# One wo stripe loaded as 96 partitions over all DMA engines and four times 8 partitions over eight engines

## The chip, the cores and the metric

The kernel runs on one core of one Trainium2 chip. The metric is the device time of one execution in microseconds (us). Here "engine" means one of the core's 16 DMA engines, the units that move data between HBM and SBUF (the core's on-chip memory, addressed as 128 partitions); compute engines are called by name. A "row" is one contiguous packet that a DMA engine moves into one partition (in the trace a stripe is 128 packets of 9216 bytes).

## The reference

Two independent attention problems, A and B, of the same shape; the outputs are concatenated. Only the window of the last 4096 positions is read, so about 150 MB must come from HBM while the arithmetic is that of one token.

```python
B, Sq, D = 2, 1, 576
Hq, Hkv, Sk, Dh = 32, 16, 16384, 128          # W = 4096
q = (x @ wq).reshape(B, Sq, Hq, Dh).transpose(0, 2, 1, 3)
k = repeat(k_cache[:, :, Sk - W:, :], 2, axis=1)
v = repeat(v_cache[:, :, Sk - W:, :], 2, axis=1)
p = softmax(einsum("bhqd,bhkd->bhqk", q, k) * Dh ** -0.5)
o = einsum("bhqk,bhkd->bhqd", p, v)
out = o.transpose(0, 2, 1, 3).reshape(B, Sq, Hq * Dh) @ wo
```

## The kernel before

SyncE issues a fixed sequence of loads: both wq, then slabs of K and V of 4 MB each (128 partitions, 32 KB per partition) into four ring slots, and between them eight "stripes" of wo (1024 rows of the matrix, 128 partitions, 9216 bytes per partition) into two buffers. A load waits only for the last reader of its slot. The loads land in the order of issue (the first landings of four slabs queued one behind the other come at 34.42, 44.15, 53.87 and 63.57 us). The part that issues a stripe:

```python
ring = sb("ring", [128, NSLOT, SW], BF16)           # 4 x 32 KB per partition
wob  = sb("wob", [128, 2, 8, NOUT], BF16)           # 2 x 9216 bytes per partition
# ... cut ...
def issue(key):
    kind, i = key
    if kind == "W":
        P, gl = i // GP, i % GP
        sl = i % 2
        rows = probs[P][4][gl * 1024:(gl + 1) * 1024, :].rearrange("(p j) n -> p j n", j=8)
        deps = [proj_op[i - 2]] if i >= 2 else []
        cuts = [(0, 8, wo_sem[sl])]
        # ... cut: the last two stripes go in two and three column pieces ...
        stream_dma[key] = []
        for j0, j1, sm in cuts:
            def f(e, j0=j0, j1=j1, sm=sm):
                return e.dma_start(wob[:, sl, j0:j1, :].rearrange("p j n -> p (j n)"),
                                   rows[:, j0:j1, :].rearrange("p j n -> p (j n)")).then_inc(sm, 16)
            stream_dma[key].append((j0, j1, dma_op("sp", sm, 1, f, deps, "wo%d_%d" % (i, j0))))
        return
    # ... cut: the same for a slab of K or V into ring[:, r] ...
```

## Time and profile before

| | before |
|---|---|
| median, 6 runs beside the change | 363.61 us (363.37 to 366.12) |
| bytes read from HBM | 153.1 MB, 422 GB/s over the span |
| share of 16 DMA engines' time, SyncE's ring | 98.7% |
| TensorE / VectorE busy | 65% / 58% |
| 16 landings of the 432 KB piece of the last stripe | 357.76 to 359.92 us |

From the page of the kernel before: the span, compute busy times, the DMA share and rate in 40 slices (a 9 is 90% or more), the queue that SyncE feeds and one of the two that fetch instructions (packets, MB, share of 16 engines), the chain of waits by engine, and the full wo loads of problem A (KB each, median us from issue to landing).

```profile
span 362.4 us, 2626 instructions
...
PE 235.4 (65%) x1296; PEld 57.1 (16%) x928; DVE 211.9 (58%) x141; ACT 46.3 (13%) x80; POOL 21.9 (6%) x82
...
DMA  8999999999999999999999999999999999999996
GB/s 326 448 428 420 445 421 438 430 423 445 412 443 430 427 441 406 443 434 430 435 421 438 430 427 436 423 434 434 427 427 433 430 438 423 436 427 434 416 412 245
...
q1 hardware_dynamic: 6772, 153.10, 98.7%
q8 instruction: 8, 0.13, 0.1%
...
DMA 60%; DVE 24%; PE 8%; issue 6%; ACT 1%; SPq 0%; POOL 0%
...
wob<-in_A_wo_dram SPq DMA_DIRECT2D x4, 1152.0 KB, 30.8
```

The DMA engines are busy all the time and everything else has slack. So the time is bytes over rate, or, more exactly, what the slowest of the 16 engines needs, plus about 2.5 us of tail.

The stretches around stripe 1, which runs through the engines at 144 to 147 us. The columns are named in the first line: busy us (and instructions) of each compute engine, granted TensorE clock, DMA share and GB/s. Single lines of this view further down have the same columns.

```profile
core 0: us, PE busy (x) PEld busy (x) DVE busy (x) ACT busy (x) POOL busy (x), PEclk, DMA share, GB/s
130.00:141.00 11.00, 7.14 (x25) 1.51 (x14) 9.26 (x8) 0.00 (x0) 0.39 (x2) 0.84 1.00 430
141.00:152.00 11.00, 7.72 (x64) 2.22 (x48) 6.17 (x4) 5.01 (x8) 1.27 (x4) 0.96 1.03 436
152.00:163.00 11.00, 8.21 (x22) 1.46 (x11) 6.72 (x3) 0.00 (x0) 0.00 (x0) 0.66 1.00 429
163.00:350.00 187.00, 123.76 (x737) 32.48 (x568) 115.73 (x83) 25.47 (x41) 9.36 (x34) 0.85 1.00 429
```

Three steps of the chain of waits, in order of time (start, us, what): the same kind of slab takes 27 to 29 us from issue to landing every time, because two or three slabs are always queued ahead of it.

```profile
99.17 27.28 DMA ring<-in_A_k_cache_dram
...
139.24 28.85 DMA ring<-in_B_k_cache_dram
...
180.88 28.86 DMA ring<-in_B_k_cache_dram
```

The trace also has each DMA packet (start, duration, bytes; not the engine) and each landing on a semaphore, 16 for a load of 128 rows; each is read as one engine's share. From these records of the kernel before:

```
row of 32768 bytes   1.213 to 1.225 us (5th to 99th percentile)   26.9 GB/s
row of  9216 bytes   0.347 to 0.360 us (5th to 99th percentile)   26.4 GB/s
instruction fetch, 16384 bytes   8 packets of 1.02 to 1.10 us, at 47, 103, 144, 185, 226, 268, 310, 339 us
instruction fetch,  8192 bytes   3 packets of 0.31 to 0.33 us
landings of one slab on its 16 engines: spread 0.65 us (44.15 to 44.79) early, 2.20 us (347.43 to 349.63) late
```

The instruction fetches go through the same 16 engines as the data and put an engine about 1.05 us behind for the rest of the run: after the first one, at 47 us, the spread of a slab's landings goes from 0.64 to 1.67 us and stays there (1.69 us at 104 us) until the next fetch, at 103 us, has run. That is the imbalance that the change seems meant for.

### The profile page before, as it was taken

Reading aid. Unit: us, or ns where it says so; the run is one execution under the profiler, and the core shown is the slowest. Engines: PE = TensorE matmul, PEld = TensorE weight load, DVE = VectorE, ACT = ScalarE, POOL = GpSimd, SP = SyncE. Lnnn points to the kernel's source line nnn. Section 1 sums busy time; section 2 is a strip of 40 time slices with the busy share of each in tenths; the row PEclk is TensorE's granted clock in tenths of the full one; section 3 lists DMA queues with packets and bytes.
Section 4 is the critical chain, followed back from the end, with each engine's and each line's share of the span. In section 5 each row is a group of like instructions: output and inputs, shape, how many; then the busy total and the mean of one; then the engine's idle time right before and its main releaser. Section 6 shows DMA issues by size and latency. Waiting matters only on the chain.

```text
span 362.4 us, 2626 instructions
## 1 busy us (share of the span) xinstructions
PE 235.4 (65%) x1296; PEld 57.1 (16%) x928; DVE 211.9 (58%) x141; ACT 46.3 (13%) x80; POOL 21.9 (6%) x82
## 2 busy tenths in 40 slices
PE   0397698566666856665786737657686646668566
PEld 0010111112111211111121201212121111212212
DVE  0201899495949093954939185582929467493622
ACT  1002100140041000500032000500005000400500
POOL 3100101100010001000010000100010001000000
PEclk9999699969897889868698977998888898978879
DMA  8999999999999999999999999999999999999996
GB/s 326 448 428 420 445 421 438 430 423 445 412 443 430 427 441 406 443 434 430 435 421 438 430 427 436 423 434 434 427 427 433 430 438 423 436 427 434 416 412 245
DMA packets 6803, 153.26 MB, mean 423 GB/s; under 512 B 764, under 2 KB 904, under 8 KB 1544
## 3 DMA queue, kind: packets, MB, share of 16 engines
q1 hardware_dynamic: 6772, 153.10, 98.7%
q8 instruction: 8, 0.13, 0.1%
q14 instruction: 3, 0.02, 0.0%
q10 hardware_dynamic: 20, 0.01, 0.0%
HBM read 153.10 MB, written 0.00 MB: 422 GB/s over the span
## 4 chain that ended last, share of the span: by engine, by line
DMA 60%; DVE 24%; PE 8%; issue 6%; ACT 1%; SPq 0%; POOL 0%
DMA ring<-in_B_k_cache_dram 32%; DVE xt L427 15%; DMA ring<-in_A_k_cache_dram 14%; DMA ring<-in_B_v_cache_dram 8%; DMA ring<-in_B_wq_dram 7%; PE st L244 2%; DVE oR L559 2%; DVE mx L461 2%; PE st L453 2%; DVE pT L500 2%; PE pj L244 2%; DVE tmp L552 2%; ACT pR L491 1%; PE pj L608 1%; DVE oP L583 1%
## 5 line engine op out<-in xcount | busy, mean ns | idle before, releaser
L453 PE MATMUL st<-xt,zq 128*128 128x512 bf16 x256 | 122.5, 478 | 92.2 <-DVE xt L427 92.2
L427 DVE STREAM_TRANSPOSE xt<-ring 128x4096 f32<-128x4096 f32 x32 | 141.6, 4430 | 39.1 <-DMA ring<-in_A_k_cache_dram 23.8
L244 PE MATMUL st<-xt,zq 128*128 128x512 bf16 x256 | 121.2, 474 | 0.0
L491 ACT ACTIVATE pR<-st,bias 128x512 bf16<-128x512 f32 x32 | 40.1, 1422 | 226.7 <-DVE bias L484 226.7
L453 PEld LDWEIGHTS st<-xt,zq 128*128 128x128 bf16 x256 | 29.0, 113 | 215.1 <-DVE xt L427 109.0
L530 PE MATMUL ot<-ring,pT 128*32 128x512 bf16 x512 | 32.6, 396 | 6.4 <-DMA ring<-in_B_v_cache_dram 6.4
L484 DVE SCALAR_TENSOR_TENSOR bias<-vmask,tb,offm 128x4 f32<-128x4 f32 x8 | 1.8, 223 | 36.6 <-PE tb L481 36.6
L514 DVE TENSOR_REDUCE ssum<-tb 128x2 f32<-128x8 f32 x8 | 1.3, 161 | 37.1 <-PE tb L511 37.1
L500 DVE STREAM_TRANSPOSE pT<-pR 128x2048 bf16<-128x2048 bf16 x8 | 18.4, 2304 | 1.2 <-ACT pR L491 1.2
L419 POOL TENSOR_TENSOR zq<-qs,bmask 128x64 bf16<-128x64 bf16 x32 | 8.7, 294 | 165.8 <-PE st L244 143.6
L552 DVE SCALAR_TENSOR_TENSOR tmp<-ot,rsb,dmask 128x512 f32<-128x512 f32 x16 | 11.5, 717 | 8.7 <-PE ot L530 8.7
L559 DVE TENSOR_REDUCE oR<-tmp 128x128 f32<-128x512 f32 x15 | 15.7, 1044 | 0.5
L530 PEld LDWEIGHTS ot<-ring,pT 128*32 128x32 bf16 x512 | 12.4, 99 | 21.7 <-DMA ring<-in_B_v_cache_dram 8.5
L608 PE MATMUL pj<-wob,oP 128*2 128x288 bf16 x64 | 15.1, 286 | 0.0
L244 PE MATMUL pj<-wob,oP 128*2 128x288 bf16 x56 | 14.0, 286 | 0.0
L244 PE MATMUL pj<-ring,pT 128*32 128x512 bf16 x36 | 11.5, 402 | 0.0
L254 PE MATMUL tb<-ident_b,pR 8*128 8x8 bf16 x9 | 0.7, 198 | 14.2 <-DVE pR L215 14.2
L461 DVE TENSOR_REDUCE mx<-st 128x2 f32<-128x1024 f32 x8 | 9.7, 1214 | 0.0
L491 ACT ACTIVATION_READ_ACCUMULATOR pR<-st,bias 128x1 f32 x32 | 9.1, 285 | 0.0
L275 PE MATMUL ot<-ring,pT 128*32 128x512 bf16 x18 | 7.3, 405 | 1.3 <-DMA ring<-in_B_wq_dram 0.9
L215 DVE TENSOR_TENSOR pR<-tmp,hmask 8x1152 bf16<-8x1152 bf16 x1 | 1.3, 1347 | 11.2 <-DMA tmp<-in_B_x_dram 11.2
L565 PE MATMUL tb<-oR,selx 128*128 128x256 f32 (+1 forms) x18 | 5.9, 408 | 2.7 <-DVE ssum L514 1.5
(64 smaller groups left out, 68.8 us busy)
## 6 DMA issues: line engine op xcount, KB each, us to landing
ring<-in_A_k_cache_dram SPq DMA_DIRECT2D x8, 4096.0 KB, 27.9
ring<-in_A_v_cache_dram SPq DMA_DIRECT2D x8, 4096.0 KB, 30.5
ring<-in_B_k_cache_dram SPq DMA_DIRECT2D x8, 4096.0 KB, 28.9
ring<-in_B_v_cache_dram SPq DMA_DIRECT2D x7, 4096.0 KB, 30.5
ring<-in_A_wq_dram SPq DMA_DIRECT2D x1, 4608.0 KB, 13.6
ring<-in_B_wq_dram SPq DMA_DIRECT2D x1, 4608.0 KB, 24.1
wob<-in_A_wo_dram SPq DMA_DIRECT2D x4, 1152.0 KB, 30.8
wob<-in_B_wo_dram SPq DMA_DIRECT2D x2, 1152.0 KB, 30.2
```

Source lines behind the costliest of these rows:

```text
L244: return e.add_instruction(mybir.InstMatmult(name=nc.get_next_instruction_name(), engine=mybir.EngineType.PE, ins=[e.lower_ap(mv_), e.lowe ...
L275: last = e.matmul(QB[c], wt, mv_, start=first, stop=True, skip_group_check=True)
L419: last = e.tensor_tensor(dst, src, msk, ALU.mult)
L427: Xop[(t, jh)] = dve(lambda e: e.transpose(xt[:, jh, :].bitcast(FP32).rearrange("p (kp x kt) -> p x kp kt", kp=2, kt=2), ring[:, r, jh * H ...
L453: last = e.matmul(ob, wt, mv_, start=first, stop=True, skip_group_check=True)
L461: ch[(G, "max")] = dve(lambda e: e.tensor_reduce(mx[:], st[:, :].rearrange("p (x t) -> p t x", t=2), AX.X, ALU.max), [Sop[(2 * G + 1, 1)]] ...
L491: last = e.activation(pR[:].rearrange("p (x k) -> p k x", k=4)[:, kv, :], st[:, :].rearrange("p (x t) -> p t x", t=2)[:, kv % 2, :], ACTF.Exp,
L500: pT_op[G] = dve(lambda e: e.transpose(pT[:, v, :].rearrange("p (w j q) -> p j w q", w=4, q=8), pR[:].rearrange("p (j w q) -> p j w q", w= ...
L530: last = e.matmul(OTB[32 * c:32 * c + 32, :], pT[:, v, base + 32 * c:base + 32 * c + 32], ring[:, r, jj * 128:(jj + 4) * 128], start=rd == ...
L552: evac_op[i] = dve(lambda e: e.scalar_tensor_tensor(tv, o, rsb[:, v, b:b + 1], dm, ALU.mult, ALU.mult), deps, "ev%d" % i)
L559: ch[(G, "red%d" % b)] = dve(lambda e: e.tensor_reduce(oR[:, b, :], tmp[:].rearrange("p (j d) -> p d j", j=4), AX.X, ALU.add), [evac_op[i] ...
L608: last = e.matmul(PJ[h], wt, mv_, start=start and j == 0, stop=True, skip_group_check=True)
```

## The change

Stripe 1 is dealt unevenly: 6 rows to each of 16 engines and 4 more to each of eight, instead of 8 to each. That is an estimate from the landings, 16 for a load of 128 rows and eight for one of 8 rows (t1_tags), with each load taken as dealt evenly; no trace names the engine of a row. One half of the engines is relieved of two rows (0.69 us), the other half gets two more.

```diff
                 stream_dma[key] = []
+                if i == 1:
+                    halves = [(0, 96)] + [(96 + 8 * k, 104 + 8 * k) for k in range(4)]
+                    def f(e, sm=wo_sem[sl]):
+                        for p0, p1 in halves:
+                            last = e.dma_start(wob[p0:p1, sl, :, :].rearrange("p j n -> p (j n)"),
+                                               rows[p0:p1, :, :].rearrange("p j n -> p (j n)")).then_inc(sm, 16)
+                        return last
+                    stream_dma[key].append((0, 8, dma_op("sp", wo_sem[sl], len(halves), f, deps, "wo%d" % i)))
+                    return
                 for j0, j1, sm in cuts:
```

## The prediction

> **What bounds the kernel.** The DMA engines. The slice view shows DMA at 9 tenths nearly throughout; in the queue view SyncE's ring takes 98.7% of 16 engines' time. 153.1 MB in 362.4 us is 422 GB/s. Single packets agree: a 32 KB row takes 1.213 to 1.225 us (26.9 GB/s), a 9216-byte row of wo 0.347 to 0.36 us, each beginning as the last ends. The chain of waits is DMA for 60%; two or three 4 MB transfers are always outstanding (28 to 30 us to landing, 9.7 us of engine time each). So the time is that of the slowest of 16 engines, plus about 2.5 us of tail.
>
> **Imbalance.** Landings of a transfer on its 16 engines spread over 0.65 us at the start and over 2.15 us for the last wo piece (357.76 to 359.92 us). The growth comes from instruction fetches: eight packets of 16 KB, 1.02 to 1.10 us each, put one engine after another about 1.05 us behind for good; three of 8 KB cost 0.31 us each. From the phase of A's output transfer I infer that neither of the two engines it uses is among the eight.
>
> **What the change does.** Before: 8 rows per engine. After: 6 rows on each of 16 engines, then four more on eight of them. [...] plus and minus 2 x 0.347 = 0.69 us. [...] Four more issues (0.59 us each) hide in SyncE's 7 us wait for a slot.
>
> **The other side.** [...] Every engine is busy to the end, so lost time is not regained.
>
> **Prediction.** 366.6 us; range 363.4 to 371. [...] Faster by over 2%: 0.01; within 2%: 0.91; slower by over 2%: 0.08.
>
> **Right if:** rows of the four small transfers take well over 0.36 us (0.7 to 2), eight engines leave the stripe 3 to 6 us late, landings of later transfers spread over 4 to 6 us instead of 2 and the last landing is 2 to 5 us later with compute unchanged.
> **Wrong if:** those rows still take 0.35 us (then the final spread shrinks to about 1.5 us, the time by about 0.5); [...] or run-to-run variation (363.5 to 366.1) hides it all.

Where the text above is marked as cut, it rested on statements about the hardware that no trace or run here shows: which eight engines an 8-row load uses, and why its rows should take longer. The sum came to 366.6 us. It weighed two cases, both estimates: about 363.8 us (30%) if the rows of the small transfers keep their time, and 366 to 369 us (70%) if they slow each other. For the second, the author had the eight engines of the small transfers lose 3 to 5 us, less about 1 us that they were thought to have in hand. The guess (65%): the engines put behind by fetches are those which the small transfers leave alone; then the last landing was to fall by about 0.5 us, otherwise to come 0.7 us later.

(What the prediction calls "the last wo piece" is the 432 KB piece of the last stripe; a piece of 144 KB lands 0.36 us after it.)

## The result and the profile after

The changed kernel takes 368.76 us in the median of 6 runs (368.32 to 370.87), the kernel before 363.61 us. The ratio is 1.0136, 95% interval 1.0100 to 1.0171: slower, but within 2%. A ratio here is the mean time of one kernel's fast runs over that of the other's of the same rounds, so it is not quite the ratio of the medians quoted.

The same lines of the page after:

```profile
span 367.2 us, 2629 instructions
...
PE 233.9 (64%) x1295; PEld 57.0 (16%) x928; DVE 211.9 (58%) x141; ACT 46.3 (13%) x80; POOL 22.0 (6%) x82
...
DMA  8999999999999999999999999999999999999995
GB/s 322 450 428 421 436 452 403 453 421 439 421 444 414 443 421 355 301 446 414 444 408 454 414 450 421 441 414 446 418 415 449 436 421 446 412 446 421 418 413 224
...
q1 hardware_dynamic: 6804, 153.10, 98.6%
...
DMA 60%; DVE 23%; PE 8%; issue 6%; ACT 1%; SPq 0%; POOL 0%
...
wob<-in_A_wo_dram SPq DMA_DIRECT2D x3, 1152.0 KB, 28.6
```

DMA is as busy as before, compute is busy for the same time, the bytes are the same. Only the rate has a hole: the 16th and 17th slice (about 138 to 156 us) fall to 355 and 301 GB/s.

The same stretches as before:

```profile
core 0: us, PE busy (x) PEld busy (x) DVE busy (x) ACT busy (x) POOL busy (x), PEclk, DMA share, GB/s
130.00:141.00 11.00, 7.20 (x24) 1.44 (x13) 9.37 (x8) 0.00 (x0) 0.39 (x2) 0.84 0.99 427
141.00:152.00 11.00, 6.34 (x59) 1.95 (x45) 4.71 (x3) 4.99 (x8) 1.27 (x4) 1.00 1.03 273
152.00:163.00 11.00, 8.16 (x28) 1.64 (x15) 8.17 (x4) 0.00 (x0) 0.00 (x0) 0.85 1.00 429
163.00:350.00 187.00, 120.30 (x704) 31.35 (x535) 114.19 (x81) 25.44 (x41) 9.39 (x34) 0.84 1.00 430
```

Between 141 and 152 us the core received 273 GB/s instead of 436, at an unchanged DMA share of 1.03. The missing 163 GB/s over 11 us are 1.8 MB, which take 4.2 us at 430 GB/s. From 163 to 350 us the rate is that of before (430 against 429). So the whole loss happens once, while stripe 1 goes through, and is never made good. A "busy" DMA engine need not be one that moves data at its full rate.

The chain of waits shows it as one step. The slab issued at 139.3 us took 33.05 us instead of 28.85; the steps beside it are as before.

```profile
99.40 27.15 DMA ring<-in_A_k_cache_dram
...
139.34 33.05 DMA ring<-in_B_k_cache_dram
...
185.18 29.08 DMA ring<-in_B_k_cache_dram
```

The five issues of SyncE, from the timeline (start, us, engine, line, what). They take 1.99 us together, and SyncE then waits for a slot until 126.22 us in any case.

```profile
119.87 1.99 SPq L358 DMA_DIRECT2D wob<-in_A_wo_dram  x5
...
126.22 0.54 SPq L381 DMA_DIRECT2D ring<-in_A_v_cache_dram  x1
```

The packet and landing records after:

```
rows of 9216 bytes of stripe 1, in order of their start:
  the first 96 (the 96-row transfer)     middle half 0.60 to 0.71 us, only 5 of 96 below 0.40
  the last 32 (the 8-row transfers)      middle half 0.78 to 0.92 us, up to 1.01
32 KB rows right behind them    up to 2.99 us (1.22 undisturbed)
landings, 432 KB piece of the last stripe   361.32 to 364.63 us (before: 357.76 to 359.92)
landings of stripe 1 on its semaphore   52, of which 4 come at once, at 121.0 to 122.0 us
```

The last line is read so: the four early entries come over 20 us before the first row of the stripe moves (143.59 us), one for each small transfer, and no row brought them (what wrote them is not shown). That leaves 48: 16 for the 96 rows and eight for each small transfer, so each ran on eight engines. An 8-row load with a semaphore of its own shows eight landings too (t1_tags, below). Of the sixteen landings late in the run, the first moved by 3.56 us and the last by 4.71 us. All engines lost, not eight.

### The profile page after: what moved, and what is told of

It is laid out like the page before. It is cut to its first block, busy times and chain, and to the rows that moved or that the text cites. A ratio compares the mean times of both kernels' runs of the same rounds, so it can differ in the third digit from the quotient of the medians.

```text
span 367.2 us, 2629 instructions
## 1 busy us (share of the span) xinstructions
PE 233.9 (64%) x1295; PEld 57.0 (16%) x928; DVE 211.9 (58%) x141; ACT 46.3 (13%) x80; POOL 22.0 (6%) x82
## 4 chain that ended last, share of the span: by engine, by line
DMA 60%; DVE 23%; PE 8%; issue 6%; ACT 1%; SPq 0%; POOL 0%
DMA ring<-in_B_k_cache_dram 32%; DVE xt L436 14%; DMA ring<-in_A_k_cache_dram 14%; DMA ring<-in_B_v_cache_dram 8%; DMA ring<-in_B_wq_dram 7%; PE st L244 2%; DVE oR L568 2%; DVE mx L470 2%; PE st L462 2%; DVE pT L509 2%; PE pj L244 2%; DVE tmp L561 2%; ACT pR L500 1%; PE pj L617 1%; DVE oP L592 1%
## 5 line engine op out<-in xcount | busy, mean ns | idle before, releaser
L462 PE MATMUL st<-xt,zq 128*128 128x512 bf16 x256 | 121.1, 473 | 98.7 <-DVE xt L436 98.7
L244 PE MATMUL st<-xt,zq 128*128 128x512 bf16 x256 | 119.9, 469 | 0.0
L509 DVE STREAM_TRANSPOSE pT<-pR 128x2048 bf16<-128x2048 bf16 x8 | 18.4, 2304 | 1.2 <-ACT pR L500 1.2
```

The costliest lines, as they stand in the source:

```text
L244: return e.add_instruction(mybir.InstMatmult(name=nc.get_next_instruction_name(), engine=mybir.EngineType.PE, ins=[e.lower_ap(mv_), e.lowe ...
L462: last = e.matmul(ob, wt, mv_, start=first, stop=True, skip_group_check=True)
L509: pT_op[G] = dve(lambda e: e.transpose(pT[:, v, :].rearrange("p (w j q) -> p j w q", w=4, q=8), pR[:].rearrange("p (j w q) -> p j w q", w= ...
```

## The experiments

Three explanations were put against each other. **P**: the destination partitions decide; rows that go to some sets of partitions slow each other and the rows of the queue beside them. **K**: a transfer that is not the plain 128-row one, or runs on eight engines, or the larger number of transfers, is slow in itself. **S**: the source rows in HBM collide.

The author chose the sets, and reckoned P's figures in the expectations, from an assumption about the hardware that no trace or run here shows. The words "home", "foreign", "crowded" and "even" in the labels are left over from it. No trace names the engine of a packet. So which eight engines carry an 8-row load is not shown; that the same eight carry all of them is assumed below. Where rows per engine are counted (six of 96, two of 32, one of 16), even dealing is assumed.

All results in one table. "Last landing" is that of the 432 KB piece in the profiled run, against 359.92 us in the profile of before; it is free of the tail's variation, which is told at the end. "Rows" is the middle half of the durations of the altered or extra rows, the parts of a stripe told apart by order of start. All runs gave the right result and are of fast state, except that t1_tags, a single run, has no state. Each last landing and each row duration comes from one profiled run; e5_cols5 and t1_tags, which change nothing that matters here, lie within 0.2 us of before.

| run | median us, beside before's | ratio (95%) | last landing | rows, us |
|---|---|---|---|---|
| the change | 368.76, 363.61 | 1.0136 (1.0100 to 1.0171) | +4.71 | 96: 0.60 to 0.71; 8: 0.78 to 0.92 |
| e5_cols5 | 365.04, 364.22 | 1.0017 (0.9959 to 1.0074) | -0.05 | 2304 bytes: 0.093 to 0.106 (5th to 95th percentile) |
| e1_96_32 | 367.85, 363.52 | 1.0128 (1.0104 to 1.0152) | +3.30 | 96: 0.57 to 0.70; 32: 0.59 to 0.63 |
| e2_spread8 | 369.98, 363.52 | 1.0173 (1.0133 to 1.0213) | +4.23 | 96: 0.59 to 0.67; 8: 0.71 to 0.78 |
| d3_home | 364.99, 363.52 | 1.0040 (1.0024 to 1.0057) | +1.03 | 0.347 to 0.349 |
| d2_foreign | 367.42, 363.51 | 1.0072 (1.0012 to 1.0132) | +2.71 | 0.68 to 0.71 |
| d1_crowded | 367.93, 363.52 | 1.0123 (1.0106 to 1.0140) | +4.54 | 0.83 to 0.90 |
| d8_16home | 365.99, 364.22 | 1.0042 (0.9990 to 1.0093) | +1.13 | 0.347 |
| d9_16even | 369.44, 364.22 | 1.0127 (1.0066 to 1.0188) | +3.94 | 0.63 to 0.70 |
| d5_96 | 368.47, 364.22 | 1.0129 (1.0068 to 1.0189) | +4.64 | 0.61 to 0.65 |
| t1_tags | 365.89 (one run), 363.51 | none | -0.18 | |

### Is it the number of transfers? (e5_cols5)

Stripe 1 in five transfers, each of all 128 partitions and some of the columns.

```diff
+                cols = [0, 2, 4, 6, 7, 8]
+                if i == 1:
+                        for a, z in zip(cols, cols[1:]):
+                            last = e.dma_start(wob[:, sl, a:z, :].rearrange("p j n -> p (j n)"),
+                                               rows[:, a:z, :].rearrange("p j n -> p (j n)")).then_inc(sm, 16)
```

> Stripe 1 as five transfers, as in the change, but each of all 128 partitions and a part of the columns. If the number of transfers, their issue or their completions cost: a good part of plus 4.9 us. Theory P: plus 0.05 to 0.2 us, rows at 27 GB/s.

The last landing did not move (-0.05 us), and the rate in the stretch of stripe 1 is nearly that of before:

```profile
141.00:152.00 11.00, 7.77 (x65) 2.33 (x49) 6.20 (x4) 5.00 (x8) 1.27 (x4) 0.98 1.03 425
```

Five issues and five completions cost nothing that can be seen here. This part of K falls. (A row of 2304 bytes in 0.093 to 0.106 us is 22 to 25 GB/s, less than the 27 expected, which is the rate of 32 KB rows (26.9).)

### Without the 8-row transfers (e1_96_32)

```diff
-                    halves = [(0, 96)] + [(96 + 8 * k, 104 + 8 * k) for k in range(4)]
+                    parts = [slice(0, 96), slice(96, 128)]
```

> Stripe 1 as 96 rows and then 32 rows, both over all 16 engines: the four small transfers are gone, the 96-row one stays. Theory P [...]: plus 2.0 to 2.6 us over the kernel before, rows of the 96-row part still 0.6 to 0.7 us. Theory K (a transfer on eight engines is slow or unbalanced in itself, whatever its partitions): within 0.3 us of the kernel before. Theory S (the source rows read from HBM are what collides): like the changed kernel for the 96 rows, so plus 1 to 2 us as well; it is told from P by the pair of extra-load runs.

It was slower by more than any of the three had it: +3.30 us at the last landing, where P's reckoning gave 2.0 to 2.6. Both transfers are meant for all 16 engines (six and two rows each), so the uneven dealing and the eight engines are not the main cost of the change. The 96-row transfer does most of the damage here: its 96 rows took 63 us of engine time in all instead of 33 (96 x 0.347), the 32 rows 19 instead of 11. The stretch of stripe 1:

```profile
141.00:152.00 11.00, 6.22 (x59) 1.86 (x45) 4.42 (x2) 4.98 (x8) 1.26 (x4) 0.93 1.02 290
```

### The small transfers to every fourth partition (e2_spread8)

```diff
-                    halves = [(0, 96)] + [(96 + 8 * k, 104 + 8 * k) for k in range(4)]
+                    parts = [slice(0, 96)] + [slice(96 + k, 128, 4) for k in range(4)]
```

> The change with one thing altered: the four 8-row transfers take partitions 96+k, 100+k, ... 124+k[...]. Same engines, rows and bytes. Theory P: plus 2.2 to 3.7 us over the kernel before, 1.3 to 1.7 us less than the change (plus 4.9), and rows of the small transfers 0.6 to 0.75 us instead of up to 1.0. Theory K: the same plus 4.9 us as the change.

The rows of the small transfers took 0.71 to 0.78 us instead of 0.78 to 0.92, and the last landing came to +4.23 us instead of +4.71. The expected gain of 1.3 to 1.7 us did not come: within the change, eight neighbouring partitions rather than every fourth one are worth about half a microsecond in one profile of each, and the times (367.92 to 371.4 us) are too scattered to say even that. A miss. In both, the small transfers go to partitions 96 to 127, and the 96-row transfer is the same.

### The same extra rows to different partitions (d1_crowded, d2_foreign, d3_home)

Here the kernel before stays whole. Behind stripe 0, four 8-row loads are added which nobody reads, into the buffer that stripe 1 fills later (stripe 1 waits for them, and they have long landed). Source rows, number and size of the loads and place in the queue are the same in all three; only the destination partitions differ.

```diff
+                if i == 0:
+                    parts = [slice(96 + 8 * k, 104 + 8 * k) for k in range(4)]   # d1_crowded: eight neighbours a load
+                    parts = [slice(96 + k, 128, 4) for k in range(4)]            # d2_foreign: every fourth of 96..127
+                    parts = [slice(k, 32, 4) for k in range(4)]                  # d3_home: every fourth of 0..31
+                    def g(e):
+                        for k, p in enumerate(parts):
+                            q = slice(96 + 8 * k, 104 + 8 * k)
+                            last = e.dma_start(wob[p, 1, :, :].rearrange("p j n -> p (j n)"),
+                                               rows[q, :, :].rearrange("p j n -> p (j n)")).then_inc(extra_sem, 16)
+                        return last
+                    extra_op.append(dma_op("sp", extra_sem, len(parts), g, deps, "extra"))
```

> The kernel before, its stripe 1 whole, and four extra 8-row loads (295 KB that nobody reads) after stripe 0, into partitions 96-103, 104-111 and so on[...]. Theory P: plus 4.5 to 5.7 us, rows of 9216 bytes up to 1.0 us and more. Theory K: the same here, and also in d3_home. If neither holds and only the engines' own time counts: plus 1.4 us (4 x 0.347)[...].

> As d3_home and d1_crowded, same source rows, engines and sizes, but into partitions 96+k, 100+k, ... 124+k[...]. Theory P: rows about 0.68 us[...], plus 2.6 us: between d3_home (1.4) and d1_crowded (4.4). If only crowding among the eight counts: as d3_home.

> As d1_crowded, the same source rows, engines, sizes and place in the queue, but into partitions k, k+4, ... k+28[...]. Theory P: rows stay at 0.347 to 0.36 us; plus 0.3 us [...] to 1.4 us. Theory K or S: as d1_crowded, plus 4.5 us or more.

The stretch from 102 to 113 us, in which the extra rows go through. First the kernel before, then d3_home, d2_foreign and d1_crowded; the last two numbers of a line are DMA share and GB/s.

```profile
102.00:113.00 11.00, 6.88 (x49) 1.71 (x40) 8.29 (x5) 5.03 (x8) 1.27 (x4) 0.87 1.03 438
```

```profile
102.00:113.00 11.00, 6.88 (x48) 1.76 (x40) 8.10 (x5) 5.01 (x8) 1.27 (x4) 0.85 1.03 439
```

```profile
102.00:113.00 11.00, 6.88 (x54) 1.76 (x42) 8.31 (x5) 5.02 (x8) 1.27 (x4) 1.00 1.06 385
```

```profile
102.00:113.00 11.00, 6.88 (x54) 1.77 (x42) 8.41 (x6) 5.01 (x8) 1.26 (x4) 1.00 1.03 312
```

Every fourth partition of 0 to 31 leaves the rate where it was (439 against 438 GB/s), and every row takes its usual 0.347 us. Every fourth partition of 96 to 127 doubles the rows to 0.68 to 0.71 us and stretches the 32 KB rows of the queue to as much as 2.4 us: 385 GB/s. Eight neighbours of 96 to 127: 0.83 to 0.90 us, 32 KB rows up to 2.9 us, 312 GB/s. With source rows, shapes and number of loads the same, S and K cannot produce this; that the destination partitions decide is shown. What in the hardware makes them decide is not. The costs at the last landing, +1.03, +2.71 and +4.54 us, are close to what P had (0.3 to 1.4, 2.6, 4.5 to 5.7).

In d1_crowded the engines without extra rows lost time too: even the first of the last landings moved by 3.13 us (357.76 to 360.89), and it belongs to an engine without them, if the same eight carry them in both runs, since in d3_home it did not move (357.68). How that comes about was not tested.

### Sixteen rows to two sets of partitions (d8_16home, d9_16even)

Four extra 16-row loads, one row for each engine, otherwise as above.

```diff
+                    parts = [slice(32 + k, 96, 4) for k in range(4)]   # d8_16home: every fourth of 32..95
+                    parts = [slice(k, 64, 4) for k in range(4)]        # d9_16even: every fourth of 0..63
+                            q = slice(64 + 16 * k, 80 + 16 * k)
```

> The kernel before with four extra 16-row loads into partitions 32+k, 36+k, ... 92+k: one row an engine[...]. Theory P: rows 0.347 to 0.36 us, plus 1.4 us (4 x 0.35), landings' spread unchanged. If not being a 128-row transfer is itself what costs (theory K): plus 2.7 us or more, rows 0.6 us or more.

> As d8_16home, same source rows, engines and sizes, but into partitions k, k+4, ... 60+k[...]. Theory P: rows about 0.68 us, plus 2.7 us. Theory K or S: the same as d8_16home.

The same stretch, d8_16home and then d9_16even:

```profile
102.00:113.00 11.00, 6.88 (x47) 1.67 (x39) 6.57 (x5) 5.01 (x8) 1.27 (x4) 0.81 1.05 444
```

```profile
102.00:113.00 11.00, 6.88 (x49) 1.71 (x40) 8.00 (x5) 5.01 (x8) 1.27 (x4) 0.87 1.05 345
```

A difference of 32 partitions in the destination decides between 444 and 345 GB/s. A 16-row transfer is not slow in itself; into these partitions it is (rows 0.35 us in d8_16home against 0.68 to 0.70 us at their steadiest in d9_16even). Nor are the upper partitions slow as such: d9_16even writes to lower ones than d8_16home. d9_16even cost +3.94 us, though, where doubling four rows gives 2.7. The rest is in what follows: of the next sixteen 32 KB rows, one an engine, fourteen took about 2.1 us or more (up to 2.3) and the two that came last 1.5 to 1.7 us, instead of 1.22. Why the trouble outlasts the rows was not tested and stays open.

### The 96 rows by themselves (d5_96)

One extra 96-row load into partitions 0 to 95, otherwise as above.

```diff
+                    parts = [slice(0, 96)]
+                            q = slice(0, 96)
```

> The kernel before with one extra 96-row load (6 rows an engine, 885 KB that nobody reads) into partitions 0-95 after stripe 0. Engine time alone: plus 2.1 us (6 x 0.35), rows 0.35 us. [...] From e1_96_32, where all sixteen engines were slowed to 0.55-0.75 us a row, I expect 4.5 to 6 us, that is 2.4 us or more above engine time.

```profile
102.00:113.00 11.00, 6.88 (x54) 1.76 (x42) 8.46 (x6) 5.01 (x8) 1.27 (x4) 1.00 1.03 327
```

It cost +4.64 us at the last landing, against 2.1 us of engine time for six rows: 2.5 us are lost. The middle half of the rows took 0.61 to 0.65 us, and the 32 KB rows after them up to 2.3 us. That this transfer runs at little more than half rate (0.347 against 0.61 to 0.65 us a row) is shown. That its destination partitions are the reason here too is argued from the small loads and not shown, since no load of 96 rows to other partitions was run. How the rows are dealt to the engines, and how waiting spreads from one engine to others, stays open.

### Which engines are late? (t1_tags)

Five tiny loads of 16, 8, 4, 2 and 1 rows of 128 bytes, behind the last but one stripe, each with a semaphore of its own.

```diff
+        tagb = sb("tagb", [16, 5, 64], BF16)
+                if i == NG - 2:
+                    def g(e):
+                        for t, n in enumerate([16, 8, 4, 2, 1]):
+                            last = e.dma_start(tagb[0:n, t, :], rows[0:n, 0, 0:64]).then_inc(tag_sem[t], 16)
 ... cut: the five semaphores, and waits for them at the very end ...
```

> The kernel before with five tiny tag loads (16, 8, 4, 2 and 1 rows of 128 bytes, each row on one engine) put behind the last but one wo stripe, so that their landings tell which engines are how late at the end. [...] The time itself should be within 0.3% of the kernel before.

(If the late engines were those that an 8-row load leaves alone, the eight landings of the 8-row tag would be the early half of the sixteen.)

The landings, in us:

```
16 rows: 355.38 355.45 355.63 355.64 355.78 356.25 356.40 | 356.75 356.80 356.99 357.09 357.09 357.22 357.25 357.28 357.38
 8 rows: 355.56 355.85 355.98 356.44 356.58               | 356.98 357.20 357.45
```

Counted from the bar, nine engines are late; three of them are among the eight of the 8-row tag, six among the others. (The bar is a choice; drawn one step earlier, before 356.25 and 356.44, it has five of the eight among eleven late ones.) The eight are not the early half, and the latest of them lands with the latest of all. d3_home says the same in another way: 1.39 us more work (4 x 0.347) on the eight engines of its loads moved the last landing by 1.03 us.

The single run took 365.89 us although its last landing is 0.18 us earlier than before's. The reason is the tail, and it concerns several runs here. The kernel before and d8_16home, around the last landing; the clock is the third number from the end:

```profile
357.00:360.00 3.00, 3.00 (x29) 1.06 (x21) 0.68 (x2) 0.40 (x1) 0.00 (x0) 1.00 0.61 238
```

```profile
359.00:362.00 3.00, 3.00 (x14) 0.76 (x6) 0.37 (x1) 0.00 (x0) 0.00 (x0) 0.50 0.38 148
```

In five of the twelve profiles (e1_96_32, d2_foreign, d8_16home, d9_16even, t1_tags) TensorE was granted half the clock around the last landing, and the final projection took about 2.5 us more; that the kernel before does so too in some executions is inferred from its times (runs at 363.4 and at 366.1 us): from the last landing to the end it is 2.5 us in the kernel before (362.4 less 359.92) and 5.0 in d8_16home (366.1 less 361.05). For that reason the last landing is the better measure of a difference of a microsecond, and the ratios of d2_foreign, d8_16home, d9_16even, e2_spread8 and e5_cols5 have wide intervals.

## Why the prediction was right, and where it was not

- **What bounds the kernel, and that lost DMA time is not regained: right.** The rate is 430 against 429 GB/s in the 187 us after the disturbance, and the +4.2 us of one step of the chain reach the end.
- **Direction and time: right within the range.** 366.6 us predicted (363.4 to 371), 368.76 measured. That rows of such small loads can take twice their time and more, the case given 70%, is shown by d1_crowded and d2_foreign (0.83 to 0.90 and 0.68 to 0.71 us) against d3_home (0.347), and by d9_16even (0.63 to 0.70) against d8_16home (0.347): the destination partitions decide. Why they do was an assumption, and was not shown. That the sum came out in the range is in part luck: it left out what the 96-row transfer loses, and a term put a longer time on each row of the small transfers than the 0.78 to 0.92 us that they took.
- **The term that was mis-sized** is the loss on the eight engines of the small transfers (3 to 5 us, less about 1 us in hand). Together that is 2 to 4 us; the last landing moved by 4.71, and the loss lay elsewhere. First, the prediction reckoned with the four 8-row transfers and let the 96-row one pass as "6 rows on each of 16 engines". That transfer alone cost 2.5 us above its engine time (d5_96), and with a 32-row one instead of the small ones the stripe is already at +3.30 of the change's +4.71 us. All 16 engines paid, so the spread of the last landings became 3.31 us and not 4 to 6. Second, little was in hand: three of the nine late engines are among the eight of the 8-row tag (t1_tags), and 1.39 us of work on these engines moved the last landing by 1.03 us (d3_home), which leaves 0.36 us and not about 1.
- **That the small transfers leave the late engines alone (65%): wrong.** The late ones are on both sides (three and six in t1_tags), so the change would not have gained even with rows of 0.347 us. From d3_home, 0.69 us more on the eight engines would put the last landing about 0.3 us later (0.69 less the 0.36 in hand; an estimate). The inference from the two engines of A's output (two packets of 1152 bytes, at 276.32 and 276.36 us), that neither was late by then, was too little to go by.
- **"Rows of the four small transfers take well over 0.36 us (0.7 to 2)": right, at the low end** (middle half 0.78 to 0.92). Of "eight engines leave the stripe 3 to 6 us late" the size is right, the eight are not: all sixteen did (+3.56 us at the first of the last landings, +4.71 at the last).
- **Eight engines for an 8-row transfer: right** (eight landings for the 8-row tag of t1_tags, and eight for each small transfer as the 52 entries were read). Which eight no trace shows.
- **Four more issues are hidden: right** (1.99 us of issues, then a wait until 126.22 us; e5_cols5 moved the last landing by -0.05 us).

## What to carry to other kernels

In a kernel bound by DMA, look at the destination partitions of a load as well as at its rows per engine: here a 16-row load ran at half rate into one set of partitions (d9_16even: rows of 0.68 to 0.70 us) and at full rate 32 partitions higher (d8_16home: 0.347), and the slow one held up the transfers queued behind it (32 KB rows of up to 2.3 us instead of 1.22). A load of all 128 partitions did not have this (0.347 to 0.360 us a row), one of partitions 0 to 95 did (0.61 to 0.65, d5_96). A high DMA busy share does not tell the two apart (1.03 at 438 GB/s before, 1.03 at 312 in d1_crowded); the rate in the same stretch and the duration of single rows do. Before shifting work from slow engines to fast ones, find out which are which, for instance by a tiny load that uses some of them only.
